# Attention followed by a channel mix: q and k of six batches turned by transposing DMAs, not by the matrix engine

## The chip, the cores and the metric

The kernel runs on one core of a Trainium2 chip. The metric is the device time of one execution in microseconds. An execution reads all inputs from the chip's main memory (HBM) and writes the whole output there. The core has a matrix engine (TensorE, PE in the profile, with its weight loads as PEld), VectorE (DVE), ScalarE (ACT), GpSimd (POOL) and SyncE (SP). SP and POOL issue the DMAs here; 16 DMA engines carry them out.

## The reference

Eight batches, eight heads, 576 tokens, 64 channels a head. First causal attention in a sliding window of 128 tokens with a linear position bias, then a channel mix with a gate:

```python
def _attn_ref(q, k, v):
    ...
    scores = scale * np.matmul(q, k.transpose(0, 1, 3, 2))
    ...
    mask = (rel >= 0) & (rel < window)
    scores = np.where(mask, scores + bias[None], -1000000000.0)
    ...
    return np.matmul(attn, v).astype(np.float32)

def _moe_ref(x, mu_k, mu_r, w_k, w_v, w_r):
    ...
    xk = mu_k * x + (1.0 - mu_k) * x_prev
    xr = mu_r * x + (1.0 - mu_r) * x_prev
    k = np.maximum(xk @ w_k, 0.0)
    v = k * k @ w_v
    r = 1.0 / (1.0 + np.exp(-(xr @ w_r)))
    return (r * v).astype(np.float32)
```

`x` is the attention's output with the heads side by side (512 wide), `x_prev` the same one token earlier, `d_ff` is 1024. Inputs and output are float32; the kernel computes in bfloat16 and accumulates in float32.

## The kernel before

**Tiles.** A batch's 576 tokens are four blocks of 128 and a tail of 64. Two heads make a pair, of 128 partitions (2 x 64 channels) when q and k are turned; there are 32 pairs, `it` = 4 x batch + pair. Since the window is 128 tokens, a block of keys meets only its own block of queries and the next.

**Attention of a pair.** q and k must come with channels on the partitions, while a load brings tokens there. `load_ql` brings half a batch of q or k, four tokens in a row to a partition (1 KB pieces read, 512 bytes written, cast to bfloat16 by POOL's DMA). `by_token` (VectorE) regroups one pair, `qk_transp` turns its eight blocks on the matrix engine (line 135) into PSUM, `qk_copy` (ScalarE, line 115) brings them to SBUF. The tails of q and k of a batch come by `load_tail`, are turned by `tail_transp` (line 148) and copied by `tail_copy`. `scores` is done in two halves (line 187), `expo` is the exponential (line 195), `masked` multiplies by bias and mask (line 200), `av` multiplies by v and a column of ones (line 218), `norm` divides, `x_transp` and `x_copy` turn the result, and `mix` makes `xk` and `xr`. For the four pairs of batch 0 the bias goes into PSUM by an extra matmul (line 176).

**Channel mix.** Two batches make a unit `P` of 1152 rows, worked in stripes of columns: `mm1` (line 268) with `relu` and `square`, `mm3` (line 287) with `gate`, `mm2` (line 302) with `product` (line 308), and a store of 128 rows by SP.

**Order.** All five engines run a fixed list. `op(...)` declares a step with its engine, an assumed duration and what it needs; `plan()` puts the steps out in the order of their assumed times; and the lists in `ORDER` fix, for PE, ACT and DVE, which step follows which. The steps' names are used below: `tq.9` are the transposes of pair 9, `pq.9` their copy, `ct.9` the regrouping, `tail.2` the tail of batch 2, `score.16.0` a half of the scores of pair 16 (the first pair of batch 4), `m1`, `m3`, `m2a` and `m2` the matmuls of the channel mix, `oo` the product. An engine waits at a step whose input is not there; it doesn't go on to the next one. A part of the PE list:

```python
score.15.1 av.13 tq.17 m1.1.0.3 score.16.0 m2a.0.8 score.16.1 m1.1.0.2 ot.13 m2.0.8
...
m3.1.2 m3.1.0 m2a.1.2 score.20.0 ot.16 score.18.1 m2.1.2 m2a.1.1 score.19.0 m1.1.512.0
```

POOL's list is the order of declaration: batch by batch half of q and k, the tails, five tiles of v, the other half of q and k, with the weights in front of batch 2. q and k have two buffers, v and the tails three, products three.

Of the kernel before, what the change touches and what calls it, by code (L numbers as in the profile page):

```python
# [17 lines left out]
def kernel(  # L18
# [32 lines left out]
    NHW = 2  # L51
    RELU_SCALE = 0.5 ** 0.5
# [25 lines left out]


# [86 lines left out]
    def scores(it, e):  # L166
        early = it < NEARLY
        b, g = divmod(it, G)
        qk, tt = qk_buf[it % NBUF], tt_buf[b % 2]
# [9 lines left out]
        for (u, q0, n) in pieces:  # L179
            c0 = BASE[u] + q0 - 128 * u - a0  # L180
            for hl in range(2):
                r = 64 * hl
                kk_ = (qk[r:r + 64, 1, 128 * u:128 * u + 128] if u < NF else
                       tt[r:r + 64, g, 0:2].rearrange("p t c -> p (t c)"))
                qq_ = (qk[r:r + 64, 0, q0:q0 + n] if q0 < SM else
                       tt[r:r + 64, g, 2, q0 - SM:q0 - SM + n])
                nc.tensor.matmul(sa[:, hl, c0:c0 + n], lhsT=kk_, rhs=qq_,  # L187
                                 start=not early, stop=True, skip_group_check=True)
# [56 lines left out]
    def mix(it, which):  # L245
# [9 lines left out]
        else:  # L255
# [3 lines left out]
            scalar=(muk_sb, mur_sb)[which][:, g:g + 1], in1=xp, op0=ALU.mult, op1=ALU.add)  # L259
# [46 lines left out]
    def product(P, c):  # L306
        ot = otp.tile([128, DM], FP32, tag="ot", name="ot")
        nc.vector.scalar_tensor_tensor(  # L308
            out=ot, in0=T.pop(("rs", P, c)), scalar=1.0, in1=T.pop(("pv", P, c)),
            op0=ALU.add, op1=ALU.mult)  # L310
        nc.sync.dma_start(out=of[SP * P + 128 * c:SP * P + 128 * c + 128, :], in_=ot)
# [11 lines left out]
    muk_sb = cst.tile([128, NPO], FP32, name="muk_sb")  # L323
    mur_sb = cst.tile([128, NPO], FP32, name="mur_sb")
# [41 lines left out]
    nc.vector.memset(tt_buf[0][:, :, 1], 0.0)  # L366

# [10 lines left out]
    LAG = {"PE": 250, "ACT": 180, "DVE": 130, "POOL": 130}  # L378
# [3 lines left out]
    def op(name, eng, busy, run, deps=(), pri=0, alloc=None, uses=(), dma=0):  # L382
        o = dict(name=name, eng=eng, busy=busy, run=run, deps=list(deps), pri=pri,
                 alloc=alloc, dma=dma, done=None, seq=len(ops), not_before=0)
# [8 lines left out]
    def plan():  # L393
# [3 lines left out]
        while any(lists.values()):  # L397
            best = None
            for eng, todo in lists.items():
# [3 lines left out]
                for o in (todo[0:1] if eng in ("SP", "POOL") else todo):  # L403
# [39 lines left out]
            else:  # L443
                o["done"] = t + o["busy"] + LAG[o["eng"]]
# [4 lines left out]
    def add_pair(it):  # L449
# [4 lines left out]
        war = [("score", it - NBUF, h) for h in range(2)] if it >= NBUF else []  # L454
        if b == 0:
# [23 lines left out]
            if g == 0:  # L479
                op(("tail", 0), "PE", 230, lambda: tail_transp(0), [("lts", 0, i) for i in range(2)],  # L480
                   n, "mm")
                op(("tcopy", 0), "DVE", 500, lambda: tail_copy(0), [], n, uses=[("tail", 0)])
            ready = [("pq", it), ("pk", it), ("dcopy",), ("sid",)]
            vdep = [("lvt",)] + [("lvh", g // 2, j) for j in range(NF)]
# [49 lines left out]
    def add_units(P, c0, c1, pri):  # L534
# [25 lines left out]
        for c in range(c0 // 128, c1 // 128):  # L560
# [12 lines left out]
               uses=[("rs", P, c), ("m2a", P, c)])  # L573
            KKFREE[-1].append(("m2", P, c))
# [3 lines left out]
    def load_mu(i):  # L578
        with nc.allow_non_contiguous_dma("tiny mu vectors"):
            nc.sync.dma_start(out=(muk_sb, mur_sb)[i],  # L580
                                in_=(moe_mu_k, moe_mu_r)[i].rearrange("(po p) -> p po", p=128))

    KKFREE, LASTUSE, OUTS, MU = [], {}, [], [("lmu", 0), ("lmu", 1)]
# [3 lines left out]
            tk.0 tq.0 tail.0 tq.1 tk.1 score.0.1 score.0.0 tq.2 score.1.1 score.1.0 ava.0 tq.3  # L587
            av.0 score.2.1 score.2.0 ava.1 av.1 ot.0 score.3.0 ava.2 ot.1 score.3.1 av.2 av.3 ot.2
            ot.3 tq.4 m1a.0.0.0 tail.1 m1.0.0.0 score.4.0 score.4.1 m1.0.0.6 m1.0.0.4 tq.5
            m1.0.0.5 m1a.0.0.1 av.4 score.5.0 m1.0.0.1 m1.0.0.7 ot.4 score.5.1 m1.0.0.3 tq.6  # L590
            m1.0.0.2 m3.0.2 score.6.1 score.6.0 tq.7 m3.0.1 av.5 m3.0.0 m3.0.3 score.7.0 ot.5
            m2a.0.1 av.6 tq.8 m2.0.1 score.7.1 tail.2 tq.9 m2a.0.0 score.8.0 m2a.0.2 ot.6
            score.8.1 m2.0.0 score.9.0 m2a.0.3 av.7 tq.10 score.9.1 m2.0.2 ot.7 score.10.1 m2.0.3
            tq.11 av.8 score.10.0 m1.0.512.0 m1.0.768.0 score.11.1 ot.8 tail.3 score.11.0
            m1.0.768.4 m1.0.512.5 tq.12 m1.0.512.6 m1.0.768.1 m1.0.768.6 av.9 m3.0.5 tq.13
            m1.0.512.2 m1.0.512.1 m3.0.4 ot.9 score.12.0 m1.0.512.7 m1.0.768.5 score.12.1
            m1.0.512.3 tq.14 av.10 m1.0.512.4 m3.0.8 m1.0.768.2 ot.10 av.11 m2a.0.5 tq.15
            score.14.0 m2.0.5 m1.0.768.7 ot.11 m2a.0.4 score.15.0 av.12 m1.0.768.3 tq.16
            score.13.0 m2.0.4 score.13.1 m3.0.6 m1.1.0.0 ot.12 tail.4 score.14.1 m1.1.0.6 m3.0.7
            score.15.1 av.13 tq.17 m1.1.0.3 score.16.0 m2a.0.8 score.16.1 m1.1.0.2 ot.13 m2.0.8  # L600
            score.17.0 av.14 m1.1.0.4 m2a.0.6 score.17.1 tq.18 m2.0.6 m1.1.0.5 ot.14 av.15 m2a.0.7
            tq.19 m2.0.7 m1.1.0.1 score.19.1 m3.1.1 av.16 ot.15 score.18.0 m1.1.0.7 tq.20 tail.5
            m3.1.2 m3.1.0 m2a.1.2 score.20.0 ot.16 score.18.1 m2.1.2 m2a.1.1 score.19.0 m1.1.512.0
            tq.21 av.17 m2.1.1 score.20.1 m1.1.512.2 av.18 m1.1.512.3 m2a.1.0 ot.17 m1.1.512.6
            score.21.0 m2.1.0 tq.22 m3.1.3 m1.1.512.1 tail.6 ot.18 av.19 score.21.1 m2a.1.3 tq.23
            m2.1.3 score.22.1 m1.1.896.0 score.22.0 ot.19 m1.1.512.4 m3.1.6 av.20 m1.1.896.6
            score.23.0 m3.1.5 m1.1.512.5 tq.24 m3.1.4 m1.1.896.1 score.23.1 ot.20 m1.1.512.7
            m3.1.7 score.24.0 m1.1.896.7 m1.1.896.2 tq.25 av.21 tail.7 m2a.1.4 m2a.1.5 m2a.1.6
            score.25.1 ot.21 m2.1.5 m2.1.4 score.25.0 m2.1.6 tq.26 m1.2.0.0 m3.1.8 m1.1.896.5
            av.22 m1.2.0.6 m1.1.896.3 score.24.1 score.26.1 m1.2.0.3 m1.1.896.4 ot.22 av.23  # L610
            m1.2.0.2 tq.27 m3.2.3 score.26.0 m3.2.2 m3.2.1 score.27.1 m1.2.0.5 ot.23 m1.2.0.1
            m2a.1.7 av.24 m2.1.7 tq.28 score.27.0 m1.2.0.4 m1.2.0.7 score.28.1 m2a.1.8 score.28.0
            ot.24 m2.1.8 m3.2.0 av.25 av.26 m1.2.512.0 tq.29 m2a.2.0 m1.2.512.2 m2a.2.1 m2.2.0
            m2.2.1 ot.25 m1.2.512.7 m1.2.512.1 m1.2.512.4 m1.2.512.6 m3.2.5 score.29.0 tq.30
            m2a.2.3 m2a.2.2 m2.2.3 m3.2.4 ot.26 m2.2.2 score.30.0 tq.31 av.27 m1.2.896.0
            m1.2.512.3 m3.2.6 av.28 m1.2.896.7 m3.2.7 m1.2.512.5 m1.2.896.3 m1.2.896.2 ot.27
            m2a.2.4 score.31.0 m2.2.4 m1.2.896.4 score.29.1 m2a.2.6 m1.2.896.6 m2a.2.5 m2.2.6
            m2.2.5 av.29 score.31.1 m3.2.8 ot.28 m1.2.896.1 m1.2.896.5 m1.3.0.0 score.30.1 m2a.2.8
            m1.3.0.2 m2.2.8 av.30 m1.3.0.3 av.31 ot.29 m1.3.0.5 m3.3.1 m1.3.0.1 m1.3.0.6 ot.30
            m2a.2.7 m1.3.0.4 m2.2.7 m3.3.3 ot.31 m3.3.0 m1.3.0.7 m3.3.2 m2a.3.3 m2a.3.2 m2.3.3  # L620
            m2.3.2 m1.3.512.0 m2a.3.0 m2a.3.1 m2.3.0 m2.3.1 m1.3.512.3 m1.3.512.7 m1.3.512.2
            m1.3.896.0 m3.3.6 m1.3.896.1 m1.3.512.1 m1.3.512.6 m3.3.4 m1.3.896.7 m3.3.5 m1.3.512.5
            m1.3.512.4 m1.3.896.2 m1.3.896.4 m1.3.896.3 m3.3.8 m3.3.7 m1.3.896.6 m2a.3.6 m2a.3.4
            m2a.3.5 m2.3.6 m2.3.4 m2.3.5 m1.3.896.5 m2a.3.8 m2a.3.7 m2.3.8 m2.3.7
        """,
        "ACT": """
            pq.0 mask0.2 pq.1 mask0.4 mask0.6 mask0.0 exp.0.1 exp.0.0 pq.2 exp.1.1 exp.1.0 pq.3
            exp.2.1 exp.2.0 xt.0 exp.3.0 xt.1 exp.3.1 xt.2 xt.3 pq.4 rl.0.0.0 exp.4.0 exp.4.1
            rl.0.0.6 pq.5 rl.0.0.4 rl.0.0.5 exp.5.0 rl.0.0.7 xt.4 rl.0.0.1 exp.5.1 pq.6 rl.0.0.3
# [198 lines left out]
```

## Time and profile before

| | us |
|---|---|
| median of 3 runs (251.28 to 252.17) | 251.77 |
| the profiled execution | 251.67 |
| its span, first to last instruction | 249.9 |
| PE busy / PEld busy | 235.3 / 136.2 |
| DVE / ACT / POOL busy | 202.4 / 173.3 / 78.3 |
| mean granted clock of TensorE | 0.973 |
| software DMA queue (POOL's) | 63984 packets, 73.6% of 16 engines' span |
| hardware DMA queue (SP's) | 7328 packets, 12.4% |

An engine's busy time counts stretches in which at least one of its instructions runs; a matmul's end is modelled, so PE's share is not its share of peak. In the rows of slices the span is cut into 40 parts of 6.25 us and a digit is the busy share in tenths. A row of a group names the line, the engine, what is written and read, the count, the busy time, the mean of one in ns, and the idle time ahead of it with what ended it. A row of a window has its length, the busy time and count of each engine, the granted clock, the DMA engines' share and the GB/s written.

### The profile page before, as it was taken

What the parts mean: (1) busy time and instruction counts of PE and PEld (TensorE: products, weight loads), DVE (VectorE), ACT (ScalarE), POOL (GpSimd) and SP (SyncE); (2) the same over time, 40 slices, a digit from 0 to 9 for tenths busy, and PEclk for the clock granted to TensorE, in tenths of its full rate; (3) what the DMA queues carried; (4) which work ended last, traced back from release to release, by engine and by line L of the source; (5) the groups of instructions that cost most, each with busy time, mean ns of one, the idle gap of its engine ahead of it and who ended that gap; (6) DMA issues with size and microseconds to landing.
All of it is one profiled execution on the core that took longest, in us unless ns stands there. A gap on an engine that the chain in (4) does not pass through costs nothing.

```text
span 249.9 us, 5584 instructions
## 1 busy us (share of the span) xinstructions
PE 235.3 (94%) x2211; PEld 136.2 (55%) x2248; DVE 202.4 (81%) x427; ACT 173.3 (69%) x269; POOL 78.3 (31%) x117
## 2 busy tenths in 40 slices
PE   6696899999999999999999999999999999999993
PEld 2354555556765555556655656546566555446641
DVE  4489878999999998999989679998879777774342
ACT  3587489979997997697889669784765566506700
POOL 8899763767576600850180000000000000000000
PEclk9689599999999999999999999999999999999999
DMA  6999999999999991999198030011220201122022
GB/s 166 144 134 190 149 205 194 154 202 172 227 150 175 176 146 42 127 172 157 45 125 99 0 130 0 3 42 45 84 84 3 108 21 42 42 88 85 0 101 110
DMA packets 71338, 27.10 MB, mean 108 GB/s; under 512 B 48272, under 2 KB 66192, under 8 KB 71312
## 3 DMA queue, kind: packets, MB, share of 16 engines
q0 software_dynamic: 63984, 16.26, 73.6%
q1 hardware_dynamic: 7328, 10.49, 12.4%
q8 instruction: 17, 0.28, 0.5%
q14 instruction: 9, 0.07, 0.1%
HBM read 33.56 MB, written 9.44 MB: 172 GB/s over the span
## 4 chain that ended last, share of the span: by engine, by line
PE 91%; DVE 3%; DMA 3%; issue 1%; POOL 1%; ACT 1%; POOLq 0%
PE ps L268 26%; PE pv L302 25%; PE pr L287 12%; PE sa L187 8%; PE tp L135 6%; PE sa L218 6%; PE tp L238 4%; DMA ts<-in_k_dram 3%; PE sa L176 1%; DVE xu L230 1%; PE to L148 1%; DVE xk L257 1%; ACT xt L243 1%; PE pa L218 0%; DVE rc L229 0%
## 5 line engine op out<-in xcount | busy, mean ns | idle before, releaser
L268 PE MATMUL ps<-xk,wk_sb 128*128 128x384 bf16 (+2 forms) x376 | 73.7, 328 | 0.8 <-issue 0.4
L195 ACT ACTIVATE at<-sa 128x1024 bf16<-128x1024 f32 x64 | 65.5, 1033 | 8.6 <-PE sa L187 8.3
L302 PE MATMUL pv<-wv_sb,kk 128*128 128x512 bf16 x272 | 68.5, 380 | 1.0 <-issue 0.3
L274 ACT ACTIVATE rl<-ps 128x384 bf16<-128x384 f32 (+2 forms) x96 | 46.5, 498 | 27.9 <-PE ps L268 25.2
L268 PEld LDWEIGHTS <-wk_sb 128*128 128x128 bf16 x384 | 35.1, 99 | 23.9 <-issue 2.5
L115 ACT COPY qk<-tp 128x1024 bf16<-128x1024 bf16 (+1 forms) x32 | 30.8, 963 | 15.2 <-PE tp L135 14.4
L302 PEld LDWEIGHTS <-kk 128*128 128x128 bf16 x288 | 25.9, 98 | 26.6 <-issue 1.7
L200 DVE TENSOR_TENSOR at<-at,mask 128x1024 bf16<-128x1024 bf16 x56 | 37.4, 684 | 3.6 <-ACT at L195 3.6
L279 DVE TENSOR_TENSOR kk<-rl 128x384 bf16<-128x384 bf16 (+2 forms) x96 | 31.9, 351 | 9.1 <-ACT rl L274 8.9
L87 POOL DMA_DIRECT2D vs<-in_v_dram x28 | 24.8, 900 | 41.0 <-PE sa L218 33.1
L287 PE MATMUL pr<-wr_sb,xr 128*128 128x512 bf16 x134 | 35.7, 379 | 0.5
L308 DVE SCALAR_TENSOR_TENSOR ot<-rs,pv 128x512 f32<-128x512 bf16 x36 | 24.3, 683 | 12.1 <-PE pv L302 12.0
L243 ACT COPY xt<-tp 128x576 bf16<-128x576 bf16 x32 | 20.5, 640 | 12.4 <-PE tp L238 12.2
L257 DVE SCALAR_TENSOR_TENSOR xk<-dl,muk_sb,xt 128x576 bf16<-128x576 bf16 x32 | 26.2, 819 | 1.1
L257 DVE SCALAR_TENSOR_TENSOR xr<-dl,mur_sb,xt 128x576 bf16<-128x576 bf16 x32 | 25.7, 809 | 0.0
L293 ACT ACTIVATE rs<-pr 128x512 bf16<-128x512 f32 x36 | 21.7, 610 | 4.5 <-PE pr L287 3.9
L230 DVE TENSOR_TENSOR xu<-sa,rc 128x640 bf16<-128x640 f32 x29 | 23.9, 824 | 1.0
L187 PE MATMUL sa<-qk 64*128 64x256 bf16 (+1 forms) x256 | 23.7, 268 | 0.5 <-issue 0.2
L218 PEld LDWEIGHTS <-at 128*128 128x128 bf16 x576 | 20.9, 98 | 5.0 <-issue 1.1
L187 PEld LDWEIGHTS <-qk 64*128 64x128 bf16 x320 | 10.8, 96 | 20.9 <-issue 16.3
L218 PE MATMUL sa<-vs,at 128*128 128x65 bf16 x464 | 19.8, 194 | 0.6 <-ACT at L195 0.6
L287 PEld LDWEIGHTS <-xr 128*128 128x128 bf16 x144 | 13.3, 98 | 12.7 <-issue 0.4
(61 smaller groups left out, 219.3 us busy)
## 6 DMA issues: line engine op xcount, KB each, us to landing
out_dram<-ot SPq DMA_DIRECT2D x36, 256.0 KB, 2.1
ql<-in_q_dram POOLq DMA_DIRECT2D x15, 256.0 KB, 7.0
ql<-in_k_dram POOLq DMA_DIRECT2D x15, 256.0 KB, 8.4
vs<-in_v_dram POOLq DMA_DIRECT2D x28, 128.0 KB, 7.4
wk_sb<-in_moe_w_k_dram POOLq DMA_DIRECT2D x2, 512.0 KB, 6.9
wv_sb<-in_moe_w_v_dram POOLq DMA_DIRECT2D x2, 512.0 KB, 11.3
ldr<-in_q_dram SPq DMA_DIRECT2D x2, 256.0 KB, 3.8
ldr<-in_k_dram SPq DMA_DIRECT2D x2, 256.0 KB, 4.2
```

The lines of the kernel that those rows point to most:

```text
L115: nc.scalar.copy(out=dst, in_=src)
L187: nc.tensor.matmul(sa[:, hl, c0:c0 + n], lhsT=kk_, rhs=qq_, start=not early, stop=True, skip_group_check=True)
L195: nc.scalar.activation(out=at_half(it, e), in_=T.pop(("sa", it, e)), func=AF.Exp, scale=float(scale))
L200: nc.vector.tensor_tensor(out=at_half(it, e), in0=at_half(it, e), in1=mask[:, 2 * g:2 * g + 2, 256 * e:256 * e + 512], op=ALU.mult)
L218: nc.tensor.matmul(pa[:, hl, W * (t - t0):W * (t - t0) + W], lhsT=at[:, lo:lo + 128], rhs=vs[:, u, 2 * g + hl, :] if u < NF else tvb[:, 2 ...
L230: nc.vector.tensor_tensor(out=T["xu", it][:, t0:t1].rearrange("p t h d -> p h t d"), in0=a5[:, :, :, 0:D], in1=rc[:, :, 0:n, None].to_broa ...
L257: nc.vector.scalar_tensor_tensor(out=T["xk" if which == 0 else "xr", P][:, g, S * e:S * e + S], in0=dl, scalar=(muk_sb, mur_sb)[which][:, ...
L268: nc.tensor.matmul(ps[:, 0:c1 - c0], lhsT=wk_sb[:, po, 128 * fo:128 * fo + 128], rhs=xk[:, po, c0:c1], start=(po == 0), stop=(po == NPO - 1))
L274: nc.scalar.activation(out=rl[:, 0:c1 - c0], in_=T.pop(("ps", P, c0, fo))[:, 0:c1 - c0], func=AF.Relu, scale=RELU_SCALE)
L279: nc.vector.tensor_tensor(out=T["kk", P, c0][:, fo, 0:c1 - c0], in0=rl[:, 0:c1 - c0], in1=rl[:, 0:c1 - c0], op=ALU.mult)
L287: nc.tensor.matmul(pr, lhsT=T["xr", P][:, po, 128 * c:128 * c + 128], rhs=wr_sb[:, po], start=(po == 0), stop=(po == NPO - 1))
L302: nc.tensor.matmul(pv, lhsT=kk[:, fo, o:o + 128], rhs=wv_sb[:, fo], start=(fo == 0), stop=(fo == NFO - 1))
```

## The change

For batches 2 to 7 (`NXB = 2`) q and k are loaded in token rows, one DMA for each of four blocks of 128 tokens and for each of q and k, with the cast to bfloat16 (256-byte pieces read, 128 bytes written), and SP then issues a transposing DMA from SBUF to SBUF for each of q and k, and one each for their tails. `tq`, `pq`, `ct`, `tail` and `tcopy` fall away for these batches, and `scores` reads the turned blocks from `qt_buf`, in which a pair's blocks lie 512 columns apart. The q and k buffers are two as before; the second one lies in the memory of `ldr`.

Other steps move too. The tail of batch 0 is loaded as float32 by SP and cast by ScalarE (`ctail`). The mu vectors come as rows and are turned by one matmul (`tmu`, `cmu`). v of batch 0 comes in whole tiles. `dist` and the small memsets come ahead of POOL's loads. The stores become steps of their own on SP (`st`), which now has a written list as well. The lists of PE, ACT and DVE are new.

```diff
+    NXB = 2
...
+    tqk = cst.tile([128, H, D], FP32, name="tqk")
+    qt_buf = [cst.tile([128, 2 * G * SM], BF16, name=f"qt{i}") for i in range(2)]
...
+    ql_buf = [
+        cst.tile([128, 2, 2, H // 2, NF * D], BF16, name="ql"),
+        ldr.rearrange("p i g h c -> p (i g h c)").bitcast(BF16).rearrange(
+            "p (w i h c) -> p w i h c", w=2, i=2, h=H // 2)]
...
+    def by_block(b):
+        return qt_buf[b % 2].rearrange("p (i j g c) -> p i j g c", i=2, j=NF, g=G)
+
+    def load_qn(b, i, j):
+        nc.gpsimd.dma_start(
+            out=qn_buf[b % 2][:, i, j].rearrange("p (h d) -> p h d", h=H),
+            in_=(q, k)[i][b, :, 128 * j:128 * j + 128, :].rearrange("h p d -> p h d"))
+
+    def cross(b, i):
+        nc.sync.dma_start(
+            out=by_block(b)[:, i].rearrange("p j g c -> p (j g) c"),
+            in_=qn_buf[b % 2][:, i].rearrange("p j c -> p (j c)"), transpose=True)
+
+    def cross_tail(b, i):
+        nc.sync.dma_start(
+            out=tt_buf[b % 2][:, :, 2 - 2 * i],
+            in_=ts_buf[b % NLD][64 * i:64 * i + 64].rearrange("p h d -> p (h d)"),
+            transpose=True)
...
+                if b >= NXB:
+                    qk = by_block(b)
+                    kk_ = qk[r, 1, u, g] if u < NF else None
+                    if q0 < SM:
+                        qq_ = qk[r, 0, q0 // 128:(q0 + n) // 128, g]
+                        to = to.rearrange("p (j c) -> p j c", c=128)
...
+                for i in range(2):
+                    op(("tr", b, i), "SP", 2000, lambda i=i: cross(b, i),
+                       [("lqn", b, i, j) for j in range(NF)] + old, n, land=2500)
+                for i in range(2):
+                    op(("trt", b, i), "SP", 1250, lambda i=i: cross_tail(b, i),
+                       [("lts", b, i)] + old[1::2], n, land=2500)
+            ready = [("tr", b, 0), ("tr", b, 1)]
...
+        if b >= NXB:
+            add_tails(b)
+            for i in range(2):
+                for j in range(NF):
...
+                        war = [("tr", b - 2, i)]
...
+                    op(("lqn", b, i, j), "POOL", 900, lambda i=i, j=j: load_qn(b, i, j), war, dma=1050)
+            add_v(b)
+            return
```

The new PE list around the first scores of batches 2, 4 and 5, and the head of SP's list:

```diff
+            m2a.0.0 av.6 m3.0.3 m2.0.0 m2a.0.2 ot.6 m2a.0.3 av.7 m2.0.2 m2a.0.1 ot.7 m2.0.3 m2.0.1
+            score.8.1 score.8.0 m1.0.512.0 m1.0.512.3 score.9.0 m1.0.768.0 score.10.0 m1.0.512.7
...
+            m1.1.0.0 m3.0.8 m1.1.0.2 av.12 m1.1.0.1 m2a.0.6 score.14.1 score.16.0 ot.12 m2.0.6
...
+            m3.1.5 ot.17 m3.1.4 m1.1.896.5 m1.1.512.2 m3.1.7 score.20.0 score.20.1 m3.1.6
...
         "SP": """
+            lq.0.0 lq.0.1 lq.1.0 lq.1.1 ltq.0 ltq.1 lmu.0 lmu.1 trt.2.0 trt.2.1 tr.2.0 tr.2.1
+            st.0.0 st.0.3 trt.3.1 trt.3.0 tr.3.0 tr.3.1 st.0.1 st.0.2 trt.4.1 tr.4.0 trt.4.0
+            tr.4.1 st.0.4 st.0.6 st.0.5 tr.5.1 trt.5.1 tr.5.0 st.0.8 trt.5.0 st.1.0 st.1.2 st.0.7
```

More of the change, by code (lines that the diff above doesn't have):

```diff
@@ L310, in product, with store @@
             op0=ALU.add, op1=ALU.mult)
[L311 removed]
+        T["ot", P, c] = ot
+    def store(P, c):
+        nc.sync.dma_start(out=of[SP * P + 128 * c:SP * P + 128 * c + 128, :],
+                            in_=T.pop(("ot", P, c)))
     ident = cst.tile([128, 128], BF16, name="ident")
@@ L402, in plan @@
                 cands = []
-                for o in (todo[0:1] if eng in ("SP", "POOL") else todo):
+                for o in (todo[0:1] if eng == "POOL" else todo):
                     t, ok = max(free[eng], o["not_before"]), True
@@ L453, in add_pair @@
         n = it
-        war = [("score", it - NBUF, h) for h in range(2)] if it >= NBUF else []
+        old = [("score", G * (b - 2) + i, h) for i in range(G) for h in range(2)] if b > 1 else []
+        war = [("score", it - 2 * G, h) for h in range(2)] if b > 1 else []
         if b == 0:
@@ L578, in load_mu, with mu_transp, mu_copy @@
     def load_mu(i):
[L579 to L583, printed above, removed]
+        nc.sync.dma_start(out=mu_row[NPO * i:NPO * i + NPO],
+                            in_=(moe_mu_k, moe_mu_r)[i].rearrange("(po p) -> po p", p=128))
+    def mu_transp():
+        T["mu"] = p_mm.tile([128, 512], FP32, tag="mm", name="mu")
+        nc.tensor.transpose(T["mu"][:, 0:2 * NPO], mu_row, ident8)
+    def mu_copy():
+        nc.vector.tensor_copy(out=mu_sb, in_=T.pop("mu")[:, 0:2 * NPO])
+    KKFREE, LASTUSE, OUTS, MU = [], {}, [], [("cmu",)]
+    AVSPLIT, MASKPRI = (0, 1, 2), 6 * G
+    FIRST = ()
     AVSPLIT, MASKPRI = (0, 1, 2), 6 * G
@@ L593 @@
[L593 to L610, printed above, removed]
```

304 lines of the change are left out of this document (171 added, 133 removed).

## The prediction

> **What bounds the kernel now.** I read the page from the top: shares, the slices, then the chain of waits.
>
> ```profile
> span 249.9 us, 5584 instructions
> PE 235.3 (94%) x2211; PEld 136.2 (55%) x2248; DVE 202.4 (81%) x427; ACT 173.3 (69%) x269; POOL 78.3 (31%) x117
> ...
> PE   6696899999999999999999999999999999999993
> ...
> DMA  6999999999999991999198030011220201122022
> ...
> PE 91%; DVE 3%; DMA 3%; issue 1%; POOL 1%; ACT 1%; POOLq 0%
> ```
>
> From the fourth slice on the matrix engine is busy in every slice, and 91% of the chain that ends last lies on it: time taken off it there comes off the end, one for one, as long as what it then reads is ready. The DMA row is the other half of the picture. For the first 85 us (14 of 40 slices) the 16 engines show 9, and after about 135 us they have little to do. So the loads bound nothing now, but early they have no room to give away.
>
> The profiled execution took 251.67 us: its span of 249.9 and 1.8 around it. It lies 0.1 below the median of the runs, 251.77; the sum is made against 251.67. A difference under 0.3% (0.75 us) is about what a measurement here cannot tell from none.
>
> **Part 1, removed from the matrix engine.** The pieces of the chain, in order of time (start, us, what):
>
> ```profile
> 81.71 0.45 PE tp L135 x8
> ...
> 85.89 0.22 PE to L148 x4
> ...
> 89.26 0.45 PE tp L135 x8
> ...
> 90.57 0.32 PE sa L187 x4
> 90.89 0.97 PE pv L302 x4
> ...
> 97.33 0.55 PE tp L135 x8
> ```
>
> A pair's eight q and k transposes (L135) hold the engine 0.45 to 0.55 us, a batch's four tail transposes (L148) 0.22. Batches 2 to 7 have 24 pairs and 6 tails: 24 x 0.50 + 6 x 0.22 = 13.3 us leave the bound engine. The one transposition added for the mu vectors is one such matmul, 0.1 at most. The matmul count of the scores stays; their moving operand now steps over blocks of 128 columns, which I cost at nothing, each block being contiguous (it was 256 contiguous before). 13.3 - 0.1 = 13.2 us.
>
> ```profile
> L115 ACT COPY qk<-tp 128x1024 bf16<-128x1024 bf16 (+1 forms) x32 | 30.8, 963 | 15.2 <-PE tp L135 14.4
> L126 DVE COPY ct<-ql 128x1024 bf16<-128x1024 bf16 x30 | 14.1, 473 | 3.2 <-DMA ql<-in_k_dram 3.2
> ```
>
> 24 of the 32 evacuations (24 x 0.963 = 23.1 us of ScalarE) and 24 of the 30 regroupings (24 x 0.47 = 11.3 us of VectorE) go as well. I count them as nothing: VectorE, 202.4, falls with the matrix engine and stays below it.
>
> **Part 2, the start.** The tails and the casts at the front change queue: the tail of batch 0 is loaded by SP and cast on ScalarE (one copy, under the 0.96 of an L115 row, on an engine that waits there), dist is made ahead of the POOL loads, and v comes in whole tiles. In the rows of waits (engine, what, total, times, longest):
>
> ```profile
> PEld L148 <- DMA ts<-in_q_dram: 3.3, 1, 3.3
> DVE ct L126 <- DMA ql<-in_k_dram: 3.2, 2, 2.6
> ```
>
> The matrix engine's one long wait at the start, 3.3 us for the tail, loses its cause; what is late next is the second half of batch 0, for which VectorE waits 2.6. Bounds 0 and 3.3; I take 2.0, nearer to the upper end, because both loads move forward. It moves the loads and their readers alike. One wait is new: the second buffer of q and k is now the memory of the float32 rows of batch 0, so the loads of batch 1 must follow the four casts.
>
> ```profile
> 7.60 0.43 DVE L112 CAST cs<-ldr 128x512 bf16<-128x512 f32 x1
> ...
> 18.00 0.75 POOL L107 DMA_DIRECT2D ql<-in_q_dram  x1
> ```
>
> The last cast ends at 8.0, POOL comes to these loads at 18.0, or some 4 us earlier with its shorter list: 0.
>
> **Part 3, the loads.** POOL's rows (start, us, what) show the first or last q/k load of a batch: 46.24 begins batch 3, 58.08 batch 4 (its last is 70.73), 71.46 batch 5, 82.58 batch 6.
>
> ```profile
> 46.24 0.76 POOL L107 DMA_DIRECT2D ql<-in_q_dram  x1
> 58.08 0.76 POOL L107 DMA_DIRECT2D ql<-in_q_dram  x1
> 70.73 0.74 POOL L107 DMA_DIRECT2D ql<-in_k_dram  x1 [0.48 <-DMA ts<-in_k_dram]
> 71.46 0.75 POOL L107 DMA_DIRECT2D ql<-in_q_dram  x1
> 82.58 0.76 POOL L107 DMA_DIRECT2D ql<-in_q_dram  x1
> ...
> out_dram<-ot SPq DMA_DIRECT2D x36, 256.0 KB, 2.1
> ql<-in_k_dram POOLq DMA_DIRECT2D x15, 256.0 KB, 8.4
> vs<-in_v_dram POOLq DMA_DIRECT2D x28, 128.0 KB, 7.4
> ...
> ldr<-in_k_dram SPq DMA_DIRECT2D x2, 256.0 KB, 4.2
> ```
>
> A batch's 11 loads take (82.58 - 46.24) / 3 = 12.1 us. Landing takes 8.4, far above one load's share, so the loads stand in a queue: more work in it is more time. Two stretches by window (last column GB/s written), the first with v landing almost alone, the second with the wide q/k rows:
>
> ```profile
> 71.00:75.00 4.00, 3.95 (x57) 3.12 (x58) 3.93 (x11) 3.59 (x6) 3.33 (x5) 1.00 2.46 148
> ...
> 63.00:69.00 6.00, 5.95 (x66) 4.44 (x65) 5.90 (x18) 5.87 (x12) 3.25 (x4) 1.00 1.61 223
> ```
>
> A v tile (131 KB in 128-byte pieces) costs 131 / 148 = 0.89 us, an old q/k load (262 KB in 512-byte pieces) 262 / 223 = 1.18. The new q/k loads have the shape of a v tile: per batch 8 x 0.89 replaces 4 x 1.18, +2.4 us of queue.
>
> **Part 4, the crossings.** No row shows one. Per batch there are two of 128 rows x 16 blocks (2048 pieces of 256 bytes, 524 KB) and two of 64 rows x 4 blocks (256 pieces). By pieces, a v tile being 1024 in 0.89: 2 x 1.78 + 2 x 0.22 = 4.0 us of the 16 engines. By bytes at the wide rate: 2 x 524 / 223 + 2 x 66 / 223 = 5.3; at the narrow rate, 148: 8.0. By bytes read (an old q/k load reads 524 KB of float32 in 1.18): 2.7. If the engines had room it would be 0, against which the row of 9s speaks. (The Trainium skill, "DMA: Bandwidth & Descriptors", section "Issuing engines are not separate DMA queues", says that transfers issued by SP and by POOL interleave on the same 16 engines, and so speaks against the change too.) I take 4.0, the pieces being what the two windows differ in, with 2.7 and 8.0 as ends. The Trainium skill ("DMA: Bandwidth & Descriptors", section "Latency and other measured facts") gives 261 GB/s for a transposing DMA, "Advanced Engine Details and Errata" ("X-Bar Transpose (TRN2)") 350 to 400; by my estimate from these the four would take 4.5 or about 3.1 us, and the end would move by +1.0 or -1.8; no run here shows either figure.
>
> From issue to landing the last crossing of a batch costs between an undisturbed store (2.1) and a load on SP beside others (4.2): 3.2.
>
> **When batch 4 is ready, and when it is wanted.** Each batch that crosses adds to the queue, so batch 4, the last before the list leaves slack, is the latest. Its last q/k load landed at 70.73 + 8.4 = 79.1. In the new order v of batch 4 comes behind it: -(4 x 0.89 + 0.45) = -4.0. Three batches of finer loads: +3 x 2.4 = 7.2. The crossings of batches 2 and 3: +8.0. Its own last one: +3.2. Ready at 93.5.
>
> Wanted: `score.16.0`, the first score of batch 4, stands in the old list between `m1.1.0.3` and `m2a.0.8`, so it is the piece at 90.57. Before it the new list lacks 10 groups of q/k transposes and 3 tails (10 x 0.5 + 3 x 0.22 = 5.7); the other exchanged entries nearly cancel. Wanted at 84.9. The 2.0 of the start shifts both. The engine has nothing else it may run, since its order is written out: it idles 93.5 - 84.9 = 8.6 us, spread over batches 2, 3 and 4. Batch 5 is ready one period later, 93.5 + 12.1 + 2.4 + 4.0 = 112.0; `score.20.0`, the first of batch 5, stands in the old list behind `m2a.1.2`, which is the first row here:
>
> ```profile
> 109.31 0.86 PE pv L302 x4
> 110.17 0.32 PE sa L187 x4
> ...
> L268 PE MATMUL ps<-xk,wk_sb 128*128 128x384 bf16 (+2 forms) x376 | 73.7, 328 | 0.8 <-issue 0.4
> L302 PE MATMUL pv<-wv_sb,kk 128*128 128x512 bf16 x272 | 68.5, 380 | 1.0 <-issue 0.3
> ```
>
> The new list puts 10 groups of L268 (73.7 / 96 = 0.77) and 11 groups of four wide matmuls (0.86) ahead of it, 17.2 us, and takes 13 groups of transposes and 4 tails away, 7.4: wanted at 120.0. No stall from there on.
>
> Queues that the crossings stand in: on SP, stores of finished rows wait behind a crossing whose loads have not landed. `st.0.1` and `st.0.2` are behind `tr.3.1`; the three-buffer ring of products then holds `oo.0.4`, which stands just before `mask.12.0`, and that needs `tr.3.1` anyway. Cost 0. On POOL, the loads of batch 4 wait for `tr.2`, landed by then.
>
> **Part 5, the clock behind a stall.** Windows over the start (the last column but two is the granted clock):
>
> ```profile
> 20.00:24.00 4.00, 3.00 (x60) 2.16 (x60) 3.84 (x9) 3.04 (x5) 4.00 (x6) 1.00 1.28 193
> 24.00:28.00 4.00, 1.83 (x14) 1.61 (x16) 3.38 (x8) 1.25 (x3) 3.11 (x5) 0.59 2.31 157
> 28.00:32.00 4.00, 4.00 (x24) 1.88 (x24) 3.32 (x7) 2.93 (x4) 2.89 (x5) 0.56 2.19 154
> ```
>
> About 3 us of scattered idling was followed by a clock of 0.59 and 0.56 over 8 us, of which some 5.8 were busy: 5.8 x 0.43 = 2.5 us lost. Only the loss behind the last stall reaches the end, the earlier ones pass in the wait for batch 4. +2.5.
>
> **Sum.** 251.67 - 13.2 - 2.0 + 8.6 + 2.5 = 247.6 us. Ends of its own: crossings 2.7 and landing 2.1 give 8.6 - 2.6 - 1.1 = 4.9 of stall, 243.9; the start at 0 adds 2.0.
>
> **Rivals.**
> *The order is met.* Queue and crossings fit into gaps that the busy digits hide, no stall: 251.67 - 13.2 - 2.0 = 236.5. For it: the loads run ahead today by more than a batch. Against it: 8.4 us from issue to landing.
> *Narrow crossings, slower than before.* If a crossing writes as the 128-byte pieces do, four cost 8.0, the stall grows by 2 x 4.0 and its landing to 4.2: 8.6 + 8.0 + 1.0 = 17.6, and 256.6 us. It decides from the point where the stall and its clock reach 15.2, that is a stall of 12.7, or 6.1 us of crossings per batch.
> *The clock stays up.* If the 8.6 us come in pieces too short for a drop, the loss of 2.5 is missing: 247.6 - 2.5 = 245.1. The row at 24 to 28 us, where no single wait was long, speaks against it. The Trainium skill ("TensorE: Matmul & The Clock Gate", Part 1) asks for an idle window of about 3.4 us before a drop, which would favour it.
> *VectorE takes over.* 202.4 - 11.3 leaves 191 busy against 235.3 - 13.2 = 222; only a stretch that VectorE fills could hold the gain back. I fold this into the middle.
>
> **How the numbers follow.** Forecast with stalls 5 to 12 us: 0.33, at 247.6, own range 244 to 251. Clock stays up: 0.10, 245.1. Order met: 0.25, 236.5, up to 241 with small stalls. Narrow crossings: 0.25, from 252.5 to 257 and more. Stalls that just eat the gain: 0.07. Faster by over 0.3%: 0.33 + 0.10 + 0.25 = 0.68; within: 0.07; slower: 0.25. The range from 237.0 to 255.5 leaves out half of the first rival's best cases and a third of the slow ones.
>
> **What would show it.** L135 with 64 matmuls instead of 256, L148 with 8, L115 and L126 with 8 and 6: Part 1. Rows "PEld L187 <- DMA qt" or an idle of several us ahead of L187 at 55 to 95 us, with a granted clock under 1.00 after it: Parts 3 to 5. Landing times of crossings at or under 4.2, and batches of loads 18 us apart: Part 4. I am wrong if PE stays at 9 through slices 9 to 15 (order met), or if the idling goes on past batch 4.

## The result and the profile after

| | before | after |
|---|---|---|
| median, us (lowest to highest) | 251.53 (249.72 to 252.17) | 267.71 (265.83 to 268.22) |
| ratio, 95% interval | | 1.0642 (1.0565 to 1.0720) |
| profiled span | 249.9 | 266.1 |
| PE busy / the rest of the span | 235.3 / 14.6 | 226.4 / 39.7 |

The change costs 16.2 us. Runs more than 1.5% above the fastest run of the same kernel are left out of all ratios. The page after, its shares, four of its slice rows, its DMA queues and the chain of waits:

```profile
span 266.1 us, 5176 instructions
PE 226.4 (85%) x2001; PEld 127.0 (48%) x2033; DVE 191.7 (72%) x393; ACT 151.6 (57%) x246; POOL 98.3 (37%) x135
...
PE   5677999904992993499959999999999999999994
...
PEclk9799999965797799599988999999999999999999
DMA  6999999999999999999999999942310220212023
...
DMA packets 135897, 34.30 MB, mean 129 GB/s; under 512 B 125112, under 2 KB 130752, under 8 KB 135872
...
DMA 43%; PE 42%; POOL 8%; issue 4%; DVE 2%; POOLq 0%; DVEq 0%; SPq 0%
```

Before, 91% of the chain lay on the matrix engine; now 42% does, and 43% lies on DMAs. The PE row has four holes, around slices 9, 13, 16 and 21, each with lower digits in the clock row beside or behind it. The DMA row shows 9 for 25 slices (166 us) instead of 14. The packets under 512 bytes have gone from 48272 to 125112.

What the matrix engine waited for (engine, what, total, times, longest), and what it did on both sides of each hole (start, us, what, idle before):

```profile
PE sa L228 <- DMA qt<-ql: 17.6, 2, 10.0
...
PE sa L228 <- DMA qt<-ldr: 4.7, 1, 4.7
...
PE ps L309 <- DVE ot L349: 2.8, 1, 2.8
```

```profile
63.56 0.50 PE L228 MATMUL sa<-qt 64*128 64x256 bf16 x4 [10.02 <-DMA qt<-ql]
...
85.68 0.93 PE L228 MATMUL sa<-qt 64*128 64x256 bf16 x8 [4.74 <-DMA qt<-ldr]
...
109.75 0.61 PE L228 MATMUL sa<-qt 64*128 64x256 bf16 x4 [7.57 <-DMA qt<-ql]
...
137.75 1.76 PE L309 MATMUL ps<-xk,wk_sb 128*128 128x384 bf16 x5 [2.80 <-DVE ot L349]
```

L228 is the scores, `qt` what the crossings write. The first three holes are the first scores of batches 2, 3 and 4: 10.02 + 4.74 + 7.57 = 22.3 us. The fourth has another cause, told below. Together 25.1 us, which is the 39.7 - 14.6 of the table.

The rows of SP (issue start, us on SP, what) and the summary for the turned q and k:

```profile
45.55 12.61 SPq L101 DMA_TRANSPOSE qt<-ql  x2
...
67.85 11.38 SPq L101 DMA_TRANSPOSE qt<-ldr  x2
79.33 1.05 SPq L355 DMA_DIRECT2D out_dram<-ot  x2
...
89.88 5.11 SPq L101 DMA_TRANSPOSE qt<-ql  x1
95.08 1.21 SPq L106 DMA_TRANSPOSE tt<-ts  x1
96.46 7.80 SPq L101 DMA_TRANSPOSE qt<-ql  x1
...
160.06 4.62 SPq L101 DMA_TRANSPOSE qt<-ql  x2
```

```profile
L101 SPq DMA_TRANSPOSE qt<-ql x6: 1839/5487/7797, 45.6 to 162.1; - x6
L101 SPq DMA_TRANSPOSE qt<-ldr x6: 2340/5472/7429, 67.8 to 170.3; - x6
...
DMA to landing us min/median/max: 4.7/12.5/14.5
```

A crossing holds SP itself for 5.5 us (median; two stores take 1.05), the second of a batch is issued only then, and each lands 12.5 us after its issue. Once the loads are over, at 160 us, the same two take SP 4.62 together, and the shortest landing is 4.7. Batch 4: q is issued at 89.88, k at 96.46, and the scores start at 109.75, 5.5 us after SP let go of k.

### The profile page after: what moved, and what is told of

Its sections match the earlier page's. It is cut to its first block, busy times and chain, and to the rows that moved or that the text cites. A ratio compares the mean times of both kernels' runs of the same rounds, so it can differ in the third digit from the quotient of the medians.

```text
span 266.1 us, 5176 instructions
## 1 busy us (share of the span) xinstructions
PE 226.4 (85%) x2001; PEld 127.0 (48%) x2033; DVE 191.7 (72%) x393; ACT 151.6 (57%) x246; POOL 98.3 (37%) x135
## 4 chain that ended last, share of the span: by engine, by line
DMA 43%; PE 42%; POOL 8%; issue 4%; DVE 2%; POOLq 0%; DVEq 0%; SPq 0%
PE pv L343 15%; PE ps L309 14%; DMA ql<-in_q_dram 12%; DMA ldr<-in_q_dram 10%; PE pr L328 7%; DMA out_dram<-ot 5%; DMA wv_sb<-in_moe_w_v_dram 5%; DMA vs<-in_v_dram 4%; DMA ts<-in_q_dram 4%; DMA ql<-in_k_dram 3%; PE sa L259 2%; PE sa L228 2%; PE tp L279 2%; POOL ql L96 2%; POOL ldr L137 1%
## 5 line engine op out<-in xcount | busy, mean ns | idle before, releaser
L309 PE MATMUL ps<-xk,wk_sb 128*128 128x256 bf16 (+2 forms) x376 | 75.9, 341 | 3.5 <-DVE ot L349 2.8
L315 ACT ACTIVATE rl<-ps 128x512 bf16<-128x512 f32 (+2 forms) x96 | 45.9, 498 | 31.5 <-PE ps L309 26.1
L309 PEld LDWEIGHTS <-wk_sb 128*128 128x128 bf16 x384 | 36.8, 102 | 29.4 <-issue 7.9
L320 DVE TENSOR_TENSOR kk<-rl 128x256 bf16<-128x256 bf16 (+2 forms) x96 | 32.0, 353 | 13.9 <-ACT rl L315 13.5
L228 PE MATMUL sa<-qt 64*128 64x256 bf16 (+1 forms) x256 | 21.6, 275 | 23.0 <-DMA qt<-ql 17.6
L118 POOL DMA_DIRECT2D vs<-in_v_dram x32 | 28.3, 894 | 19.9 <-DMA ql<-in_q_dram 6.6
L228 PEld LDWEIGHTS <-qt 64*128 64x128 bf16 x320 | 11.9, 97 | 40.7 <-DMA qt<-ql 18.2
L298 DVE SCALAR_TENSOR_TENSOR xk<-dl,mu_sb,xt 128x576 bf16<-128x576 bf16 x32 | 26.2, 819 | 1.1
L334 ACT ACTIVATE rs<-pr 128x512 bf16<-128x512 f32 x36 | 21.7, 619 | 8.8 <-PE pr L328 8.7
L298 DVE SCALAR_TENSOR_TENSOR xr<-dl,mu_sb,xt 128x576 bf16<-128x576 bf16 x32 | 25.7, 813 | 0.0
L295 DVE TENSOR_TENSOR dl<-xt 128x576 bf16<-128x576 bf16 x32 | 14.5, 454 | 2.1 <-ACT xt L284 2.0
## 6 DMA issues: line engine op xcount, KB each, us to landing
ql<-in_k_dram POOLq DMA_DIRECT2D x12, 128.0 KB, 10.8
wk_sb<-in_moe_w_k_dram POOLq DMA_DIRECT2D x2, 512.0 KB, 10.8
```

The source lines that it names most:

```text
L118: nc.gpsimd.dma_start(out=vs_buf[b % NLD][:, j, :, 0:D], in_=v[b, :, 128 * j:128 * j + 128, :].rearrange("h p d -> p h d"))
L228: nc.tensor.matmul(to, lhsT=kk_, rhs=qq_, start=not early, stop=True, skip_group_check=True)
L298: nc.vector.scalar_tensor_tensor(out=T["xk" if which == 0 else "xr", P][:, g, S * e:S * e + S], in0=dl, scalar=mu_sb[:, NPO * which + g:NP ...
L309: nc.tensor.matmul(ps[:, 0:c1 - c0], lhsT=wk_sb[:, po, 128 * fo:128 * fo + 128], rhs=xk[:, po, c0:c1], start=(po == 0), stop=(po == NPO - 1))
L315: nc.scalar.activation(out=rl[:, 0:c1 - c0], in_=T.pop(("ps", P, c0, fo))[:, 0:c1 - c0], func=AF.Relu, scale=RELU_SCALE)
L320: nc.vector.tensor_tensor(out=T["kk", P, c0][:, fo, 0:c1 - c0], in0=rl[:, 0:c1 - c0], in1=rl[:, 0:c1 - c0], op=ALU.mult)
```

## What the experiments asked

The theory after these rows: the crossings are late, each a long step in series on SP behind a full set of DMA queues, and the written order turns lateness into idle time and then into a slow clock. The rivals: the small pieces in POOL's queue, the rearranged start, the hop itself whether it turns or not, and the written lists, made for cheaper crossings.

**The crossings left out, all else as in the change.** SP's steps stay in the order, but issue nothing; the scores read what lies in `qt`.

```diff
-                    op(("tr", b, i), "SP", 2000, lambda i=i: cross(b, i),
+                    op(("tr", b, i), "SP", 2000, lambda: None,
...
-                    op(("trt", b, i), "SP", 1250, lambda i=i: cross_tail(b, i),
+                    op(("trt", b, i), "SP", 1250, lambda: None,
```

> Leaves out: the four transposing DMAs of each of batches 2 to 7; their scores read what batches 0 and 1 left in the buffers, and no longer wait for any load of q and k. Theory A (the matrix engine's 13.2 us were really saved, and the crossings gave them back as stalls ahead of the scores): the idle stretches of 10.0, 4.7 and 7.6 us ahead of L228 vanish, and the time is 251.5 - 13.2 = about 238 us, up to 240. Theory B (taking the transposes off the matrix engine is worth little, something else bounds): over 246 us. For the queue: if the finer loads alone stretch it, a batch of loads still takes about 21 us as in the changed kernel; if the crossings do, it goes to 12.1 + 2.4 = 14.5 us.

Measured 236.29 (235.4 to 238.13), ratio 0.9425 (0.9366 to 0.9484). Its page, and its PE row for `score.16.0`, the first score of batch 4 (as at 109.75 in the change, the five transposes of `ot.12` follow it):

```profile
span 233.3 us, 5095 instructions
PE 218.6 (94%) x2001; PEld 124.0 (53%) x2033; DVE 191.3 (82%) x393; ACT 151.1 (65%) x246; POOL 98.6 (42%) x135
...
PE   6489699998999999999999999999999999999992
...
PEclk9999999999999999999999999999999999999999
```

```profile
83.45 0.38 PE L228 MATMUL sa<-qt 64*128 64x256 bf16 x4
```

No hole and no slow clock. So all that the change loses, 267.7 - 236.3 = 31.4 us, comes with the crossings: in the spans 32.8, of which 25.0 is idling (39.7 against 233.3 - 218.6 = 14.7) and 7.8 longer busy time (226.4 - 218.6) under the slower clock. The scores here no longer wait for loads either, so this run alone does not show that the finer loads are in time; the version with token-row loads below waits for them.

**Plain copies in place of the crossings.** The same bytes, queue, order and waits; what is copied is not turned.

```diff
-            in_=qn_buf[b % 2][:, i].rearrange("p j c -> p (j c)"), transpose=True)
+            in_=qn_buf[b % 2][:, i].rearrange("p j c -> p (j c)"))
```

> Leaves out the turning: SP's four transposing DMAs per batch become plain copies of the same bytes from the same buffers to the same buffers, waited for in the same way. Theory A1 (it is the transposing that is slow: many small pieces, 5 to 7.5 us to issue, 12 to 14 to land): each copy is issued in about 0.5 us and lands in 2 to 5 us, the batches' loads come about 15 us apart, the stalls ahead of the scores shrink to 5 us in all or less, 240 to 244 us. Theory A2 (any further hop through a loaded queue costs that): copies land only after 8 us or more, stalls over 15 us, 255 us or more.

Measured 247.11 (246.96 to 248.42), ratio 0.9858 (0.9811 to 0.9906): between the two expectations. The rows of the DMA issues (KB each, median us to landing), and of SP for one batch:

```profile
qt<-ql SPq DMA_DIRECT2D x6, 512.0 KB, 7.6
qt<-ldr SPq DMA_DIRECT2D x6, 512.0 KB, 7.5
```

```profile
82.44 0.49 SPq L101 DMA_DIRECT2D qt<-ql  x1
```

Both halves are real. A hop through the full queues lands after 7.6 us, though it holds SP only 0.49, and costs 247.1 - 236.3 = 10.8 us of the end, the waits for the loads themselves included. Turning costs the other 20.6. It adds 5 us on SP, and the landing comes 5 us later for that reason alone: behind the release of SP a crossing lands after 12.5 - 5.5 = 7.0 us, a copy after 7.1 (medians).

**Half the q and k loads left out, the others twice as wide,** in pieces of 1 KB read and 512 bytes written, as before the change; tokens then lie in another order.

```diff
+        if j < 2:
...
+                in_=(q, k)[i][b, 4 * j:4 * j + 4, 0:SM].rearrange("h (p r) d -> p h (r d)", p=128))
```

> Leaves the tokens in the wrong places: for batches 2 to 7 the eight DMAs per batch in token rows (256-byte pieces read) become four DMAs of the same bytes in pieces of 1 KB, as before the change; the crossings stay. Theory C (the number of pieces in POOL's queue decides: the finer loads make the batches late): stalls ahead of the scores fall to a third, under 252 us. Theory A (the crossings decide): a batch of loads takes 2 to 3 us less, 18 to 19 instead of 21.5, the crossings still take 5 us or more to issue and over 9 us to land while loads run, the stalls shrink by 3 to 8 us: 259 to 264 us.

Measured 262.42 and 262.76 in the two runs that count (266.94 and 268.38 in the others), ratio 1.0464 (1.0397 to 1.0530). That is about 5 us below the change and inside the 259 to 264 of Theory A; Theory C wanted under 252. So the pieces in POOL's queue account for a smaller part of the loss, and most of it stays without them.

**The rearranged start alone.** `NXB = 8`, no batch crosses, with the lists of before where they hold the steps.

```diff
-    NXB = 2
+    NXB = 8
```

> All of the change but the crossings (NXB = 8: every batch by wide loads and the matrix engine), with the old lists for PE, ACT and DVE and no list for SP. The prediction's 2.0 us for the start: 249.5. Rival: the second half of batch 0 and its v come no earlier, so the start gives nothing: 251 to 252 us.

Measured 253.46 (252.47 to 255.06, nine runs), ratio 1.0106 (1.0076 to 1.0137), but not a clean measure of the start: the engine waits 6.9 us at `tail.0`, which the old list puts ahead of its new, later data.

```profile
PE to L178 <- ACT ts L145: 6.9, 1, 6.9
```

**Token-row loads, turned by the matrix engine.** The same, with the change's loads, `row_transp` for `qk_transp`, and no regrouping.

```diff
+            nc.tensor.transpose(
+                tp[:, 128 * n:128 * n + 128],
+                qn_buf[b % 2][:, n // NF, n % NF, 128 * g:128 * g + 128], ident)
```

> The finer loads without the crossings: batches 2 to 7 come in token rows as in the changed kernel, and the matrix engine turns them straight from the loaded rows (no regrouping on VectorE), with the old lists. If the finer loads by themselves make batches late (14.9 us a batch instead of 12.1), stalls appear ahead of the transposes of batches 2 to 4 and the time is over 256 us; if only the crossings do, it stays within 2 us of the 253.5 of the rearrangements alone, since the matrix engine's work is what it was.

Measured 254.67 (254.23 to 255.11), ratio 1.0156 (1.0111 to 1.0201): 1.2 us above the last kernel, within the 2 us expected if only the crossings make batches late. The same wait at `tail.0` (6.5 us) is in it. POOL is busy 98.3 us instead of 74.9, yet the matrix engine waits for none of the finer loads: in this order they alone hold it up nowhere.

**Crossings by block.** Four crossings of one block each in place of one of four.

```diff
+        for j in range(NF):
+            nc.sync.dma_start(
+                out=by_block(b)[:, i, j], in_=qn_buf[b % 2][:, i, j], transpose=True)
```

> Each crossing of q or k is issued as four, one for each block of 128 tokens, so that a block can be turned as soon as its own load has landed; bytes and pieces are the same. Theory D (what stalls the scores is that SP issues two large crossings one after the other, 5 to 7.5 us each, behind the last of four loads): the last block is ready about 5 to 8 us sooner, the stalls ahead of L228 (10.0, 4.7, 7.6 us) shrink by a third to a half: 258 to 263 us. Theory E (the DMA engines are busy with the pieces themselves, whatever their order of issue): the loads still come 20.6 us a batch apart and the time stays within 2 us of 267.7.

Measured 275.83 (274.69 to 276.82), ratio 1.0997 (1.0956 to 1.1038). Both expectations missed; 8 us worse than the change.

```profile
43.37 13.50 SPq L102 DMA_TRANSPOSE qt<-ql  x8
...
158.30 11.93 SPq L102 DMA_TRANSPOSE qt<-ql  x8
```

```profile
DVE ot L349 <- DMA out_dram<-ot: 17.0, 3, 8.1
```

Eight small ones hold SP about as long as two large ones under load (13.50 against 12.61), and much longer when POOL has no more loads to issue (11.93 against 4.62). The waits for the turned blocks fall only from 22.3 to 18.0 us, and what stands behind the eight on SP's queue comes later: the matrix engine waits 7.6 us for a tail, and VectorE 17.0 for buffers that stores have to free, 6.3 in the change.

**The order planned anew,** with the crossings' measured cost, after the steps of batch 0.

```diff
-                    op(("tr", b, i), "SP", 2000, lambda i=i: cross(b, i),
-                       [("lqn", b, i, j) for j in range(NF)] + old, n, land=2500)
+                    op(("tr", b, i), "SP", 6300, lambda i=i: cross(b, i),
+                       [("lqn", b, i, j) for j in range(NF)] + old, n, land=7500)
```

> The changed kernel with the crossings' measured cost given to the planner (6.3 us to issue, 7.5 to land behind it, the loads of batches 3 to 7 at 2.0 us each), and its lists kept only up to the end of batch 0: the matrix engine's order then puts the channel mix of batches 0 and 1 ahead of the scores of batch 2. Theory F (the stalls come from an order written for loads that land sooner; the engine has other work): idling ahead of the scores falls from 25 to 8 us or less, half-speed stretches go with it, 240 to 250 us. Theory G (the loads and crossings are now themselves the bound): batches still come 20.6 us apart and the end stays over 258 us.

Measured 252.70 (252.18 to 253.04), ratio 1.0074 (1.0048 to 1.0100): 2.7 us outside the expected span, with 15.0 us of the change's 16.2 back. Its crossings and the two holes that are left:

```profile
L101 SPq DMA_TRANSPOSE qt<-ql x6: 4907/6218/6650, 44.8 to 142.8; - x6
```

```profile
63.59 0.60 PE L228 MATMUL sa<-qt 64*128 64x256 bf16 x8 [2.82 <-DMA qt<-ql]
...
69.39 1.87 PE L309 MATMUL ps<-xk,wk_sb 128*128 128x256 bf16 x8 [5.10 <-DVE ot L349]
```

The crossings are as slow as in the change, and the two holes together are 7.9 us, as Theory F has it. So the loss takes both, long steps and an order that reads them early: the new order gives back 15.0 us with steps as long as before, the plain copies 20.6 in the old order. Where the channel mix is put ahead, it fills the wait. The order doesn't remove the price of the crossings, though: 252.7 - 236.3 = 16.4 us stay against the version without them.

**Fewer batches cross, in the change.** `NXB = 4`, then 5, with the change's list for the start and the old one behind it.

> Crossings only from batch 4 on (NXB = 4): the lists of the changed kernel for batch 0, then those of the kernel before. Two thirds of the matrix engine's saving stay: 14.8 x 2/3 = 9.9 us. The loads of batch 4 are then no longer behind other crossings. If the crossings of batches 2 and 3 are what makes the later ones late, batch 4 is ready near 92 us, wanted near 89: 241 to 246 us. If the crossing's own 12 to 14 us under load are enough, stalls of 5 us or more stay and the time is 248 us or more.

Measured 259.45 (257.47 to 260.28), ratio 1.0333 (1.0274 to 1.0392): the second alternative, and over 11 us beyond its lower end. In its profile the scores wait 4.5 us for a crossing, and the matrix engine 6.3 more for a product buffer.

> Crossings only from batch 5 on (NXB = 5), lists as for NXB = 4. Saving 14.8 / 2 = 7.4 us; loads of batch 5 land near 92 us and are wanted near 108, so a crossing of 14 us fits: no stall, 243 to 246 us. If the start of the changed kernel costs something or stalls stay, over 248 us.

Measured 248.36, and 252.79 to 254.99 in three more runs, so without an interval: above the 243 to 246, and unsettled, since the profiled execution (248.36) shows no wait at the scores.

**The kernel before, with crossings for the late batches alone.** Start, lists and v loads of before; only batches from `NXB` on load token rows, after their v, and cross.

```diff
+    NXB = 5
...
+    qt_buf = [cst.tile([128, 2 * G * SM], BF16, name="qt"),
+              ldr.rearrange("p i g h c -> p (i g h c)").bitcast(BF16)]
```

> The kernel before, with crossings for batches 5 to 7 only and nothing else of the change (its start, mu loads, v halves and lists stay; the transposes of 12 pairs and 3 tails drop out of the lists). Saving 14.8 / 2 = 7.4 us. If the crossings cost only where loads fill the queue and the scores stand close behind: batch 5's loads land by about 95 us, its crossings by 108, wanted near 107: a stall of 0 to 3 us, 243.5 to 247 us. If a crossing's price does not fall with the queue: 251 us or more.

> As late_from_5 but for batches 6 and 7 only: 8 pairs and 2 tails, saving 14.8 / 3 = 4.9 us. Their loads land by 115 and 142 us, with few other loads beside the crossings; wanted near 134 and 158. If queue and distance are what decides, no stall: 246 to 247 us. If the crossings cost in themselves: 251 us or more.

> As late_from_5 but for batches 4 to 7: saving 14.8 x 2/3 = 9.9 us. Batch 4's loads land near 80 us, its second crossing some 12 to 14 us behind, wanted near 89. If the distance decides: a stall of 3 to 6 us ahead of batch 4's scores, a stretch at half clock behind it, and crossings of batch 4 that push batch 5's loads back: 245 to 250 us, no better than late_from_5. If there is still room: 241 us.

Measured from 5: 245.76 (245.2 to 246.53), ratio 0.9799 (0.9767 to 0.9832), as expected. From 6: 247.37 (245.8 to 248.08), ratio 0.9846 (0.9808 to 0.9884), just over its expected span. From 4: 255.31 (254.5 to 256.31), ratio 1.0174 (1.0137 to 1.0211), against what was expected. The rows of SP and of the matrix engine for batch 4 where crossings begin with it, then the summary of the crossings of batch 6 where they begin with 5:

```profile
76.45 4.49 SPq L94 DMA_TRANSPOSE qt<-ql  x1
83.34 6.35 SPq L94 DMA_TRANSPOSE qt<-ql  x1
```

```profile
96.82 0.61 PE L222 MATMUL sa<-qt 64*128 64x256 bf16 x4 [8.56 <-DMA qt<-ql]
```

```profile
L94 SPq DMA_TRANSPOSE qt<-ql x2: 2839/3452/4064, 114.5 to 119.8; - x2
...
DMA to landing us min/median/max: 4.5/5.8/7.1
```

One batch more, batch 4, costs 9.6 us: its crossings meet the queue at 76 to 90 us, take SP 4.49 and 6.35, and a hole of 8.56 follows. Where they begin with batch 5, at 88.95 us, POOL issues no load from 88 to 100 us; all crossings of q and k land within 7.1 us of their issue, and no score waits. This version beats both kernels, by 5.3 us against the one before and 22 against the change.

## Why the prediction was wrong

It said 247.6, with 237.0 to 255.5, and faster; it is 16 us slower, on the side of the rival "narrow crossings" and past its 256.6.

**Parts 1 and 2 together** held. Removal was put at 13.2 and the start at 2.0; without crossings the kernel gains 251.05 - 236.29 = 14.8 for both, against the 15.2 of the rival "the order is met". VectorE was no bound.

**Part 2** alone is not settled. The first matmul of the channel mix starts at 27.44 (first row) instead of 27.90 (second), which is 0.5 us and not 2.0; but behind it the clock of before is 0.56 from 28 to 32 us (the prediction's row), and 1.00 after the change. No run isolates the start.

```profile
27.44 0.38 PE L309 MATMUL ps<-xk,wk_sb 128*128 128x512 bf16 x1
```

```profile
27.90 1.06 PE L268 MATMUL ps<-xk,wk_sb 128*128 128x512 bf16 x2 [0.22 <-issue]
```

The wait for the tail went, but a wait for the second cast took its place, not the one that the prediction named:

```profile
PE tp L165 <- DVE cs L142: 3.0, 1, 3.0
```

**Part 3** held: 14.5 us per batch of finer loads. POOL's rows for the first tail load of batches 3 and 7 are 59.67 us apart without crossings, 14.9 each.

```profile
48.88 0.69 POOL L131 DMA_DIRECT2D ts<-in_q_dram  x1
...
108.55 0.77 POOL L131 DMA_DIRECT2D ts<-in_q_dram  x1
```

**Part 4** has the step that failed: the time from the issue of a batch's crossings to their landing. With crossings the same rows are 86.72 apart, 21.7 each:

```profile
48.65 0.69 POOL L131 DMA_DIRECT2D ts<-in_q_dram  x1 [0.32 <-PE tp L279]
...
135.37 0.68 POOL L131 DMA_DIRECT2D ts<-in_q_dram  x1 [1.22 <-DMA ql<-in_k_dram]
```

So a batch's crossings stretch the loads by 6.8 us, at most, since POOL's own waits are in it; 4.0 was taken, inside the ends 2.7 and 8.0. The term far outside its ends is the other one, from issue to landing of the last crossing: 3.2, between a store's 2.1 and a load's 4.2. For batch 4 it was 13.3 (96.46 to 109.75): 7.8 on SP and 5.5 behind. And it was issued only after the first crossing (5.1) and a tail (1.2), so that 19.9 us lie between the first issue, at 89.88, and the scores. The rest of Part 4 fits: by the prediction's terms the loads are ready at 93.5 - 3.2 - 2.0 = 88.3, and the first crossing, which waits for them, is issued at 89.88. Two things were overlooked. Nothing in the trace of before priced the issue itself, and the prediction put it at zero by leaving it out; two crossings run in series on SP. And neither bounding row was taken in the full queue (the median of 36 stores, most of them sent after the loads, and the first loads of all): the 8.4 us to landing of a load in the full queue stood quoted a few lines above them, and plain copies, at 7.6, show that it was the right neighbour. The Trainium skill ("Advanced Engine Details and Errata", section "X-Bar Transpose (TRN2)") says that transposing DMAs are as fast as regular ones; here the plain copies of the same 512 KB hold SP 0.49 us and land after 7.6, the crossings 5.5 and 12.5, so the measurement decides against it. The 261 GB/s of the Trainium skill ("DMA: Bandwidth & Descriptors", section "Latency and other measured facts") would give 2.0 us for one, an estimate from that page, near the 2.3 at rest (4.62 / 2) and far from the loaded 5.5. Why SP is held longer beside the loads, no run here shows.

**Ready and wanted.** Batch 4 was ready at 109.75, not 93.5, and wanted at 83.45 (the row without crossings), not 84.9 (both less 2.0 for the start). So the time at which it is wanted was forecast within 1 us, and the gap is 26.3 instead of 8.6. Behind these scores, the rest of the span with crossings (first row) and without (second), with the matrix engine's busy time after the comma:

```profile
109.75:266.10 156.35, 148.24 (x1237) 83.28 (x1258) 118.68 (x234) 89.08 (x150) 27.55 (x33) 0.98 0.82 107
83.45:233.30 149.85, 144.30 (x1245) 82.01 (x1260) 120.93 (x239) 89.09 (x151) 34.10 (x41) 1.00 0.80 90
```

The other 6.5 of the 32.8 us between the two spans are here: 3.9 longer busy time, near the 3.6 of the last two slow windows below ((3.87 + 3.39) / 2), and 2.6 more idling, near the fourth hole. That the stall is spread over batches 2, 3 and 4 held. That batch 5 meets its wish held only in the outcome, by luck: its second crossing left SP at 130.31, 18 us after the forecast 112.0, but the stalls ahead had put off its first score to 152.96.

**The queue on SP** was put at 0, and this failed too. A store that stands behind a crossing frees its product buffer late:

```profile
122.88 7.43 SPq L101 DMA_TRANSPOSE qt<-ldr  x1
130.40 0.55 SPq L355 DMA_DIRECT2D out_dram<-ot  x1
```

```profile
137.01 0.69 DVE L349 SCALAR_TENSOR_TENSOR ot<-rs,pv 128x512 f32<-128x512 bf16 x1 [4.02 <-DMA out_dram<-ot]
```

This is the fourth hole, 2.8 us: VectorE waits for the store, and the matrix engine for VectorE. The prediction had looked at `st.0.1` and `st.0.2` alone; `tr.5` and the stores behind it did the same later.

**Part 5** had the mechanism and missed the size: 2.5, for the last of the holes alone, where the busy time grew by 7.8 over all four, 3.9 of it behind the first scores of batch 4. Four windows (the last column but two is the granted clock):

```profile
55.81:69.46 13.65, 5.90 (x36) 2.69 (x37) 3.55 (x6) 3.77 (x5) 8.21 (x10) 0.50 1.93 171
83.11:89.94 6.83, 4.24 (x26) 2.72 (x28) 1.77 (x5) 3.10 (x5) 2.64 (x4) 0.50 1.83 192
107.01:113.84 6.83, 3.87 (x16) 1.73 (x18) 1.78 (x3) 2.47 (x3) 4.30 (x7) 0.50 2.07 176
137.73:141.14 3.41, 3.39 (x11) 1.49 (x11) 3.38 (x7) 0.98 (x2) 1.72 (x2) 0.50 2.74 150
```

17.4 us of busy time lie at half the clock; if all of it took twice as long, 8.7 were lost, near the 7.8. The rival "the clock stays up" fell: a hole of 2.80 was followed by the last window, right at its end. The Trainium skill ("TensorE: Matmul & The Clock Gate", Part 1) asks for about 3.4 us; here 2.80 were enough.

**The sum as it came**, in spans and in the prediction's terms: 249.9 - 16.6 (removal and start, the 233.3 without crossings; 14.8 by the medians) + 26.3 (batch 4 late) + 3.9 (the clock behind it) + 2.6 (idling behind it) = 266.1. The prediction had 15.2, 8.6, 2.5 and nothing.

## What to carry to other kernels

Price a step in the state in which it will run: a landing time from the full queue, not from the same kind of DMA at rest, and for a DMA on a queue that another one follows, its time on the issuing engine as well. A written order makes the length of a step harmless or costly; where a new step is slow, plan the order again with its measured length before judging it. Where the queue is full only for part of the run, do the exchange only in the rest: here batches 5 to 7 gained 5.3 us, and batch 4 alone took 9.6 away.

## What the hardware showed unexpectedly

- A transposing DMA of 128 x 2048 bf16 (512 KB) held SP for 1.8 us at its shortest, with POOL's loads over, and for 7.8 at its longest, beside them. A plain copy of the same bytes held it 0.49 (median). Beside the loads both landed about 7 us after SP was released (difference of the medians).
- With POOL's loads all issued, eight of 128 x 512 held SP 11.93 us, as against 4.62 for two of 128 x 2048: about 1.5 us each, gaps included, while a large one, four times the size, takes 2.3.
- A hole of 2.8 us in the matrix engine's work was followed by 3.41 us at half the clock.
